# Attention then MLP on one core: all engines in program order, an opening written by hand, and batch 2 transposed on TensorE

## The chip, the cores and the metric

One core of a Trainium2 chip. The metric is the device time of the kernel in microseconds (us), the median of several runs; executions of one kernel mostly agree within 1%. An execution more than 1.5% above the fastest of the same kernel in its call is taken as slow and left out of ratios. The granted clock is the share of PE's full clock rate that the profile shows as granted: 1.00 is full, 0.50 half; "cold" means run at less than full clock. PE is the matmul engine TensorE, DVE is VectorE, ACT is ScalarE, POOL is GpSimd (here it mostly issues the loads), SP is SyncE (it issues stores and DMA transposes).

## The reference, cut to what matters

```python
# q, k, v: (8 batches, 8 heads, 576, 64); p: (8, 8, 32, 64); x = 4608 tokens of 512
def sm_attn(qq, kk, vv): ...          # softmax(scale * qq @ kk^T) @ vv
p_packed = sm_attn(p, k, v)           # 32 packed rows per head
out = sm_attn(q, p_packed, p_packed)
x = out.transpose(0, 2, 1, 3).reshape(4608, 512)
h = x @ w_in                          # 512 -> 2048
g = s * relu(h) ** 2 + b
y = g @ w_out                         # 2048 -> 512
```

## The kernel before

The kernel works batch by batch. For each batch it prepares k, q, v and p, computes the scores of p against k ("first scores"), the packed rows ("packed"), the scores of q against the packed rows ("second scores", then "weights"), and multiplies the packed rows by w_in beforehand ("packed_w"). Then 16 hidden steps follow: `mlp_in(b, m)` is four matmuls on PE, a ReLU on ACT and a squaring on DVE into `gT`. The output tiles of a batch (16 matmuls each) are spread over the hidden steps of the next batch, and so is the attention of the batch to come. In the profile lines, `pn` is p as loaded, `pbd`, `kT` and `qT` are the transposed p, k and q, `qr` and `vr` are copies of q and v in another order that DVE makes, `ppbd` holds the packed rows, `e` exponentials, `aT` the weights, `pw` the packed rows times w_in, `hps` and `yps` are PSUM tiles, and `rlu` is what the ReLU of a hidden step gives.

Only PE's instructions are held in program order. On the other engines the scheduler may move an instruction forward when it expects its inputs to be ready.

```python
kn/qn/vn: one buffer each (rawp, bufs=1);  qr, vr, e1, e2: one each (attp, bufs=1)
kT, qT, pbd, ppbd: two each, by b % 2;     PSUM: three "h" tiles, two "y" tiles

def mm(*a, **kw):
    return tc.keep_in_program_order(nc.tensor.matmul(*a, **kw))

def by_chunk(dst, src):                      # 96 x 3072 copy on DVE
    nc.vector.tensor_copy(...)
def order_q(b): qr[b] = attp.tile(...); by_chunk(qr[b], qn[b])
def order_v(b): vr[b] = attp.tile(...); by_chunk(vr[b], vn[b])
def dma_k(b):   nc.sync.dma_start_transpose(out=kT[b % 2]..., in_=kn[b]...)
def dma_q(b):   nc.sync.dma_start_transpose(out=qT[b % 2]..., in_=qr[b]...)

def prep_p(b):
    nc.vector.tensor_copy(out=pn[:, b, :, 1, :], in_=pn[:, b, :, 0, :])   # "the p copy"
    pt = big(BF16)
    for qd in range(NQ):
        tr(pt[...], pn[:, b, qd, :, :], identb[:])                        # PE
    ...                                                                   # two copies to pbd on DVE
# ... cut: per batch b of the loop, a = b + 1, c = b + 2
    steps[11]: dma_k(c), order_q(c), dma_q(c)        # batches 3 to 7; batch 2 at steps 4 and 6 of loop 1
    steps[14]: prep_p(c), order_v(c)
    for m in range(NFF):
        mlp_in(b, m)
        for f in steps.get(m, []): f()
        if b == 1 and m < 4: ...                     # 16 bias matmuls
        run_outs(todo, per)                          # 4 or 5 output matmuls of batch b - 1
```

The softmax here doesn't subtract the row's maximum and nothing guards it: scores larger than these inputs give would overflow.

## Time and profile before

| | before |
|---|---|
| time, median of 3 runs | 316.49 us (315.71 to 317.64) |
| profiled span | 312.5 us |
| PE busy | 255.1 us (82%) |
| mean granted clock of PE | 0.944 |

A page's slices cut the span in 40; each digit is the busy share in tenths. In an answer in order of time a line has the start, the duration, the engine, the source line, the operation with its output and inputs, and in brackets how long the engine stood idle before it and for what. In a table of waits the three numbers are the sum, the count and the longest. The lines of before stand in the prediction below.

### The profile page before, as it was taken

The numbers are of one execution on the slowest core, as the hardware profiler recorded it, in microseconds if no ns is written. First come the engines' busy times: TensorE is split into PE (matmuls) and PEld (weight loads), VectorE is DVE, ScalarE is ACT, GpSimd is POOL, SyncE is SP. The second block draws the span as 40 slices with busy tenths as digits, with TensorE's granted clock in tenths as the row PEclk, the third lists the DMA queues.
The fourth block names the chain that finished last, engine by engine and source line by source line (L and its number), as shares of the span: only waits on it lengthen the run. The fifth ranks groups of instructions, "written<-read, shape, count | busy, mean of one in ns | idle before, by whom it ended". The sixth has DMA issues, their size and how long they took to land.

```text
span 312.5 us, 4756 instructions
## 1 busy us (share of the span) xinstructions
PE 255.1 (82%) x1890; PEld 144.8 (46%) x1920; DVE 146.3 (47%) x291; ACT 140.4 (45%) x209; POOL 28.8 (9%) x40
## 2 busy tenths in 40 slices
PE   0286868239599469939999799999999999999994
PEld 0272554114265236514665455556556655555441
DVE  1354845250445073436554746563665447444211
ACT  1026655402155514525547654755585467444100
POOL 8341010001101001100010000000000000000000
PEclk9999996758799959997999999999999999999999
DMA  8999999999998975986279336721112111212132
GB/s 95 203 207 202 206 196 179 144 153 176 147 180 108 185 120 107 166 125 109 64 119 182 93 88 111 150 68 35 36 34 69 34 36 34 69 36 67 47 89 67
DMA packets 59240, 35.45 MB, mean 113 GB/s; under 512 B 32081, under 2 KB 54609, under 8 KB 59217
## 3 DMA queue, kind: packets, MB, share of 16 engines
q0 software_dynamic: 25136, 18.61, 41.1%
q1 hardware_dynamic: 34080, 16.52, 27.9%
q8 instruction: 15, 0.25, 0.3%
q14 instruction: 9, 0.07, 0.1%
HBM read 37.23 MB, written 9.44 MB: 149 GB/s over the span
## 4 chain that ended last, share of the span: by engine, by line
PE 58%; DMA 10%; DVE 4%; issue 1%; DVEq 0%
PE yps L72 35%; PE hps L72 23%; DMA qT<-qr 10%; DVE gT L384 1%; DVE pw L358 1%; DVE qr L165 0%; DVE ysb L428 0%; DVE aT L333 0%; DVE vr L165 0%; PE hps L75 0%; DVE biasrep L392 0%; DVE ppbd L288 0%; DVE pbd L177 0%; DVEq L165 0%
## 5 line engine op out<-in xcount | busy, mean ns | idle before, releaser
L72 PE MATMUL yps<-w_out_sb,gT 128*128 128x512 bf16 x547 | 141.7, 387 | 5.5 <-DVE biasrep L392 3.2
L382 ACT ACTIVATE rlu<-hps 128x576 bf16<-128x576 f32 x128 | 82.9, 650 | 126.9 <-PE hps L72 125.3
L72 PE MATMUL hps<-aT,pw 128*128 128x288 bf16 x512 | 88.6, 300 | 19.1 <-DVE aT L333 12.4
L384 DVE TENSOR_TENSOR gT<-rlu 128x576 bf16<-128x576 bf16 x128 | 58.0, 455 | 77.1 <-ACT rlu L382 76.4
L72 PEld LDWEIGHTS <-gT 128*128 128x128 bf16 x576 | 53.8, 99 | 58.0 <-issue 13.9
L72 PEld LDWEIGHTS <-pw 128*128 128x128 bf16 x512 | 51.5, 102 | 58.5 <-issue 22.6
L428 DVE SCALAR_TENSOR_TENSOR ysb<-yps,svec,biasrep 128x512 f32<-128x512 f32 x36 | 26.9, 747 | 14.1 <-PE yps L72 13.8
L72 PE MATMUL hps<-w_in_sb,ppbd 128*64 128x512 bf16 x128 | 19.4, 424 | 7.4 <-DVE pbd L177 7.0
L165 DVE COPY qr<-qn 96x3072 bf16<-96x3072 bf16 x8 | 7.6, 956 | 37.6 <-DMA qT<-qr 27.5
L358 DVE TENSOR_SCALAR pw<-hps,rd 128x1024 bf16<-128x1024 f32 x16 | 20.4, 1277 | 4.4 <-PE hps L72 4.3
L252 ACT ACTIVATE e<-hps 96x768 bf16<-96x768 f32 x16 | 12.7, 799 | 15.4 <-PE hps L72 15.4
L72 PEld LDWEIGHTS <-ppbd 128*64 128x64 bf16 x192 | 9.7, 117 | 20.3 <-DVE pbd L177 7.5
L356 ACT ACTIVATE pw<-hps,rd 128x1024 bf16<-128x1024 f32 x16 | 17.8, 1114 | 0.6 <-PE hps L72 0.6
L89 POOL DMA_DIRECT2D kn<-in_k_dram x9 | 8.3, 923 | 74.8 <-DMA kT<-kn 63.4
L72 PE MATMUL hps<-pbd,kT 128*128 128x64 bf16 x192 | 9.2, 202 | 5.6 <-DVE kT L193 5.6
L316 ACT ACTIVATE e<-hps,rs 128x576 bf16<-128x576 f32 x16 | 10.9, 737 | 6.1 <-PE hps L72 5.4
L333 DVE TENSOR_TENSOR aT<-e,rcd 128x576 bf16<-128x576 bf16 x16 | 11.8, 753 | 3.9 <-ACT rcd L332 3.6
L72 PEld LDWEIGHTS <-kT 128*128 128x128 bf16 x192 | 8.6, 104 | 6.8 <-DVE kT L193 5.9
L165 DVE COPY vr<-vn 96x3072 bf16<-96x3072 bf16 x8 | 7.7, 956 | 8.2 <-DMA vn<-in_v_dram 5.8
L75 PE MATMUL hps<-identb,pn 128*128 128x128 bf16 x16 | 2.4, 239 | 10.4 <-DVE pn L172 8.6
L72 PE MATMUL hps<-e,vr 96*128 96x64 bf16 x192 | 8.8, 199 | 2.4 <-DVE qT L223 2.4
L332 ACT ACTIVATE rcd<-ld 128x576 f32<-128x576 f32 x16 | 10.6, 684 | 0.3
(41 smaller groups left out, 109.1 us busy)
## 6 DMA issues: line engine op xcount, KB each, us to landing
qn<-in_q_dram POOLq DMA_DIRECT2D x8, 576.0 KB, 8.1
vn<-in_v_dram POOLq DMA_DIRECT2D x8, 576.0 KB, 11.3
out_dram<-ysb SPq DMA_DIRECT2D x24, 192.0 KB, 2.3
kn<-in_k_dram POOLq DMA_DIRECT2D x7, 576.0 KB, 8.8
out_dram<-ysb SPq DMA_DIRECT2D x24, 128.0 KB, 2.4
w_in_sb<-in_moe_w_in_dram POOLq DMA_DIRECT2D x4, 512.0 KB, 14.0
w_out_sb<-in_moe_w_out_dram POOLq DMA_DIRECT2D x4, 512.0 KB, 21.7
out_dram<-ysb SPq DMA_DIRECT2D x24, 64.0 KB, 2.0
```

The costliest lines, as they stand in the source:

```text
L72: return tc.keep_in_program_order(nc.tensor.matmul(*a, **kw))
L89: nc.gpsimd.dma_start(out=t[:, h0:h0 + step, :], in_=src[b, h0:h0 + step].rearrange("h (r c) d -> r h (c d)", c=NC),)
L165: nc.vector.tensor_copy(out=dst[:].rearrange("r c h d -> r h c d"), in_=src[:].rearrange("r h (c d) -> r h c d", c=NC),)
L252: nc.scalar.activation(out=e1[b][:, qd].rearrange("r c g j -> r g c j"), in_=s1[0:R].rearrange("r a (g x) -> r (a g) x", g=2)[:, :, 0:NC * ...
L316: nc.scalar.activation(out=e2[b][:, qd, :].rearrange("p (a s) -> p a s", a=2), in_=tiles[qd][:, :, 0:HS], func=AF.Exp, scale=rs[b][:, qd:q ...
L332: nc.scalar.activation(out=rcd[:], in_=ld[:].rearrange("p a s -> p (a s)"), func=AF.Exp, scale=-1.0)
L333: nc.vector.tensor_tensor(out=aT[b][:, qd, :], in0=e2[b][:, qd, :], in1=rcd[:], op=ALU.mult)
L356: nc.scalar.activation(out=dst, in_=tiles[qd][:], func=AF.Copy, scale=rd[b][:, qd:qd + 1])
L358: nc.vector.tensor_scalar_mul(out=dst, in0=tiles[qd][:], scalar1=rd[b][:, qd:qd + 1])
L382: nc.scalar.activation(out=rlu[:], in_=hps[:, :, 0:HS], func=AF.Relu)
L384: nc.vector.tensor_tensor(out=gT[:, m, g0:g0 + S].rearrange("p (a s) -> p a s", a=2), in0=rlu[:], in1=rlu[:], op=ALU.mult,)
L428: nc.vector.scalar_tensor_tensor(out=ysb[:], in0=self.yps[:], scalar=svec[:], in1=biasrep[:], op0=ALU.mult, op1=ALU.add,)
```

## The change

The intent: no engine is to stand behind an instruction that the scheduler moved too far forward, the opening is to use data as they land, and batch 2, whose DMA transposes fell into the heaviest loading, is to be transposed on PE.

```diff
+    class Pinned:
+        def __getattr__(self, name):
+            f = getattr(self.engine, name)
+            return lambda *a, **kw: tc.keep_in_program_order(f(*a, **kw))
+    vec, act, pool, sp = (Pinned(e) for e in (nc.vector, nc.scalar, nc.gpsimd, nc.sync))
 # ... every nc.vector., nc.scalar.activation, nc.gpsimd., nc.sync. becomes vec., act., pool., sp.
 # ... opening, after second_scores(0):
-    weights(0, 0); weights(0, 1); packed_w(0, 0)
+    packed_w1(0, 0); weights(0, 0); weights(0, 1); packed_w1(0, 1)
+    mlp_in(0, 0..5); packed_w1(0, 2); mlp_in(0, 6..7); packed_w1(0, 3); mlp_in(0, 8..12)
+    prep_k(1, 0); prep_k(1, 1); mlp_in(0, 13); mlp_in(0, 14)
+    first_scores(1, 0); first_scores(1, 1); mlp_in(0, 15)
+    order_q(1); prep_q(1, 0); prep_q(1, 1); order_v(1); packed(1, 0); packed(1, 1)
+    loads(2)
+    with_bias(0); second_scores(1); with_bias(4); weights(1, 0); weights(1, 1)
+    packed_w(1, 0); with_bias(8); packed_w(1, 1); with_bias(12)   # each: 4 bias + 4 output matmuls
-    for b in range(B):
+    for b in range(1, B):
 # ... batch 2 in loop 1: prep_p, prep_k, order_q, prep_q, order_v on PE and DVE, steps 2 to 10
-            if b == 1:
-                at = [8, 9, 10, 11, 12, 13, 14, 14, 15]
+                at = [2, 4, 5, 6, 7, 8, 10, 11, 12, 13, 14, 14, 15]
+        if b == 2:
+            steps[1]: order_q(3), dma_k(3), dma_q(3);  steps[3]: prep_p(3), order_v(3)
-            steps[11]: dma_k(c), order_q(c), dma_q(c);  steps[14]: prep_p(c), order_v(c)
+        if b >= 2: steps[13]: order_q(c), dma_k(c), dma_q(c);  steps[15]: prep_p(c), order_v(c)
```

(The last lines and the list of calls are shortened. Left out: the loads of the batch after next now stand at step 4 of a loop, in loop 1 at step 10, instead of ahead of it; the steps of the attention in loop 2 are spread anew; 8 output matmuls stand ahead of loop 2's first hidden step.)

All instructions that go through `Pinned` show its line, L82, in the profiles after; go by the tiles there.

More of the change, by code (lines that the diff above doesn't have):

```diff
@@ L5 @@
 from concourse import bass_utils, mybir
-from concourse.masks import make_identity
 from concourse._compat import with_exitstack
@@ L75, in tr, with __init__ @@
         return tc.keep_in_program_order(nc.tensor.transpose(*a, **kw))
+    class Pinned:
+        def __init__(self, engine):
+            self.engine = engine
+        def __getattr__(self, name):
+            f = getattr(self.engine, name)
+            return lambda *a, **kw: tc.keep_in_program_order(f(*a, **kw))
+    vec, act, pool, sp = (Pinned(e) for e in (nc.vector, nc.scalar, nc.gpsimd, nc.sync))
     def big(dt=F32):
@@ L88, in load @@
         for h0 in range(0, H, step):
-            nc.gpsimd.dma_start(
+            pool.dma_start(
                 out=t[:, h0:h0 + step, :],
@@ L99, in load_p @@
     def load_p(b0, b1):
-        nc.gpsimd.dma_start(
+        pool.dma_start(
             out=pn[:, b0:b1, :, 0, :],
@@ L105, in load_w_in @@
     def load_w_in(ch):
-        nc.gpsimd.dma_start(
+        pool.dma_start(
             out=w_in_sb[:, :, ch * NB:(ch + 1) * NB],
@@ L111, in load_w_out @@
     def load_w_out(m0, m1):
-        nc.gpsimd.dma_start(
+        pool.dma_start(
             out=w_out_sb[:, m0:m1, :],
@@ L115, in load_w_out @@
         )
+    identb = constp.tile([P, P], BF16, name="identb")
+    vec.memset(identb[:], 0.0)
     load(kn, k, 0, "kn", parts=2)
@@ L119 @@
     load(qn, q, 0, "qn")
+    pool.affine_select(
+        out=identb[:], in_=identb[:], compare_op=ALU.not_equal, fill=1.0, base=0,
+        pattern=[[-1, P]], channel_multiplier=1,
+    )
     load(vn, v, 0, "vn")
     svec = constp.tile([P, 1], F32, name="svec")
-    nc.sync.dma_start(out=svec[:], in_=moe_s[0:1].unsqueeze(0).to_broadcast([P, 1]))
+    sp.dma_start(out=svec[:], in_=moe_s[0:1].unsqueeze(0).to_broadcast([P, 1]))
     bvec = constp.tile([P, 1], F32, name="bvec")
-    nc.sync.dma_start(out=bvec[:], in_=moe_b[0:1].unsqueeze(0).to_broadcast([P, 1]))
+    sp.dma_start(out=bvec[:], in_=moe_b[0:1].unsqueeze(0).to_broadcast([P, 1]))
     nc.scalar.preload_act_table_set("natural_log_exp_and_others")
-    identb = constp.tile([P, P], BF16, name="identb")
-    nc.vector.memset(identb[:], 0.0)
-    make_identity(nc, identb, nomemset=True)
     for ch in range(NCH):
@@ L139 @@
     for i in range(2):
-        nc.vector.memset(pbd[i][:], 0.0)
-        nc.vector.memset(kT[i][:, H * HS:KW], 0.0)
+        vec.memset(pbd[i][:], 0.0)
+        vec.memset(kT[i][:, H * HS:KW], 0.0)
     ones1 = constp.tile([P, 1], BF16, name="ones1")
-    nc.vector.memset(ones1[:], 1.0)
+    vec.memset(ones1[:], 1.0)
     for i in range(2):
-        nc.vector.memset(ppbd[i][:], 0.0)
+        vec.memset(ppbd[i][:], 0.0)
     onesbd = constp.tile([P, P], BF16, name="onesbd")
-    nc.vector.memset(onesbd[:], 0.0)
+    vec.memset(onesbd[:], 0.0)
     for g in range(4):
-        nc.vector.memset(onesbd[NP * g:NP * g + NP, NP * g:NP * g + NP], 1.0)
+        vec.memset(onesbd[NP * g:NP * g + NP, NP * g:NP * g + NP], 1.0)
     onesb = constp.tile([P, P], BF16, name="onesb")
-    nc.vector.memset(onesb[:], 1.0)
+    vec.memset(onesb[:], 1.0)
     biasrep = constp.tile([P, NB], F32, name="biasrep")
@@ L164, in by_chunk @@
     def by_chunk(dst, src):
-        nc.vector.tensor_copy(
+        vec.tensor_copy(
             out=dst[:].rearrange("r c h d -> r h c d"),
@@ L171, in prep_p @@
         i = b % 2
-        nc.vector.tensor_copy(out=pn[:, b, :, 1, :], in_=pn[:, b, :, 0, :])
+        vec.tensor_copy(out=pn[:, b, :, 1, :], in_=pn[:, b, :, 0, :])
         pt = big(BF16)
@@ L176, in prep_p @@
         for c2 in range(2):
-            nc.vector.tensor_copy(
+            vec.tensor_copy(
                 out=pbd[i][D * c2:D * c2 + D, :, :, c2, :],
@@ L192, in prep_k @@
                 )
-        nc.vector.tensor_copy(
+        vec.tensor_copy(
             out=kT[i][:, half * 4 * HS:(half + 1) * 4 * HS].rearrange("p (a s) -> p a s", a=2),
@@ L198, in dma_k @@
     def dma_k(b):
-        nc.sync.dma_start_transpose(
+        sp.dma_start_transpose(
             out=kT[b % 2][:, 0:H * HS].rearrange("p (x r) -> p x r", r=R),
@@ L222, in prep_q @@
                 )
-        nc.vector.tensor_copy(
+        vec.tensor_copy(
             out=qT[i][:, CP * half:CP * half + CP, :, :].rearrange("p c h r -> p (c h r)").rearrange(
@@ L230, in dma_q @@
     def dma_q(b):
-        nc.sync.dma_start_transpose(
+        sp.dma_start_transpose(
             out=qT[b % 2][:].rearrange("p c h r -> p (c h) r"),
@@ L251, in first_scores @@
                 )
-        nc.scalar.activation(
+        act.activation(
             out=e1[b][:, qd].rearrange("r c g j -> r g c j"),
@@ L287, in packed @@
             for h2 in range(2):
-                nc.vector.tensor_copy(
+                vec.tensor_copy(
                     out=ppbd[i][D * h2:D * h2 + D, :, NP * h2:NP * h2 + NP],
@@ L294, in packed @@
             rd[b] = smp.tile([P, NQ], F32, tag="rd", name="rd")
-            nc.vector.reciprocal(out=rd[b][:], in_=pp[:, 1, 0:NQ])
+            vec.reciprocal(out=rd[b][:], in_=pp[:, 1, 0:NQ])
             rs[b] = smp.tile([P, NQ], F32, tag="rs", name="rs")
-            nc.vector.tensor_scalar_mul(out=rs[b][:], in0=rd[b][:], scalar1=scale)
+            vec.tensor_scalar_mul(out=rs[b][:], in0=rd[b][:], scalar1=scale)
     def second_scores(b):
@@ L315, in second_scores @@
         for qd in range(NQ):
-            nc.scalar.activation(
+            act.activation(
                 out=e2[b][:, qd, :].rearrange("p (a s) -> p a s", a=2),
@@ L329, in weights @@
         ld = smp.tile([P, 2, HS], F32, tag="ld", name="ld")
-        nc.scalar.activation(out=ld[:], in_=dps[:, :, 0:HS], func=AF.Ln)
+        act.activation(out=ld[:], in_=dps[:, :, 0:HS], func=AF.Ln)
         rcd = smp.tile([P, S], F32, tag="rcd", name="rcd")
-        nc.scalar.activation(out=rcd[:], in_=ld[:].rearrange("p a s -> p (a s)"), func=AF.Exp, scale=-1.0)
-        nc.vector.tensor_tensor(out=aT[b][:, qd, :], in0=e2[b][:, qd, :], in1=rcd[:], op=ALU.mult)
+        act.activation(out=rcd[:], in_=ld[:].rearrange("p a s -> p (a s)"), func=AF.Exp, scale=-1.0)
+        vec.tensor_tensor(out=aT[b][:, qd, :], in0=e2[b][:, qd, :], in1=rcd[:], op=ALU.mult)
     def packed_w(b, c2):
@@ L355, in packed_w, with packed_w1 @@
             if qd == 0:
-                nc.scalar.activation(out=dst, in_=tiles[qd][:], func=AF.Copy, scale=rd[b][:, qd:qd + 1])
+                act.activation(out=dst, in_=tiles[qd][:], func=AF.Copy, scale=rd[b][:, qd:qd + 1])
             else:
-                nc.vector.tensor_scalar_mul(out=dst, in0=tiles[qd][:], scalar1=rd[b][:, qd:qd + 1])
+                vec.tensor_scalar_mul(out=dst, in0=tiles[qd][:], scalar1=rd[b][:, qd:qd + 1])
+    def packed_w1(b, ch):
+        i = b % 2
+        if ch == 0:
+            pw[b] = ppw.tile([P, NQ, DFF], BF16, tag="pw", name="pw")
+        t = big()
+        for qd in range(NQ):
+            for pr in range(2):
+                hp = 2 * qd + pr
+                mm(
+                    t[64 * pr:64 * pr + 64, qd, :],
+                    ppbd[i][:, hp, :],
+                    w_in_sb[:, hp, ch * NB:(ch + 1) * NB],
+                    start=True,
+                    stop=True,
+                    tile_position=(0, 64 * pr),
+                )
+        dst = pw[b][:, :, ch * NB:(ch + 1) * NB]
+        act.activation(out=dst[:, 0], in_=t[:, 0, :], func=AF.Copy, scale=rd[b][:, 0:1])
+        vec.tensor_scalar_mul(out=dst[:, 1], in0=t[:, 1, :], scalar1=rd[b][:, 1:2])
     def slot(b):
@@ L381, in mlp_in @@
         rlu = ysp.tile([P, 2, HS], BF16, tag="rlu", name="rlu")
-        nc.scalar.activation(out=rlu[:], in_=hps[:, :, 0:HS], func=AF.Relu)
+        act.activation(out=rlu[:], in_=hps[:, :, 0:HS], func=AF.Relu)
         g0 = slot(b) * S
-        nc.vector.tensor_tensor(
+        vec.tensor_tensor(
             out=gT[:, m, g0:g0 + S].rearrange("p (a s) -> p a s", a=2),
@@ L391, in bias_part @@
         if m == NFF - 1:
-            nc.vector.tensor_scalar_mul(out=biasrep[:], in0=cps[:], scalar1=bvec[:])
+            vec.tensor_scalar_mul(out=biasrep[:], in0=cps[:], scalar1=bvec[:])
     def store(ysb, i0, b, col, n):
@@ L400, in store @@
             m = min(R - r0, end - i0)
-            nc.sync.dma_start(out=rows[c, r0:r0 + m, :], in_=ysb[i0:i0 + m, :])
+            sp.dma_start(out=rows[c, r0:r0 + m, :], in_=ysb[i0:i0 + m, :])
             i0 += m
@@ L427, in step @@
                 ysb = ysp.tile([P, NB], F32, tag="ysb", name="ysb")
-                nc.vector.scalar_tensor_tensor(
+                vec.scalar_tensor_tensor(
                     out=ysb[:], in0=self.yps[:], scalar=svec[:], in1=biasrep[:],
@@ L454, in run_outs, with loads @@
                 todo.pop(0)
+    def loads(b):
+        load(kn, k, b, "kn")
+        load(qn, q, b, "qn")
+        load(vn, v, b, "vn")
     prep_p(0)
@@ L469, with with_bias @@
     second_scores(0)
+    packed_w1(0, 0)
     weights(0, 0)
     weights(0, 1)
-    packed_w(0, 0)
-    for b in range(B):
+    packed_w1(0, 1)
+    for m in range(0, 6):
+        mlp_in(0, m)
+    packed_w1(0, 2)
+    for m in range(6, 8):
+        mlp_in(0, m)
+    packed_w1(0, 3)
+    for m in range(8, 13):
+        mlp_in(0, m)
+    prep_k(1, 0)
+    prep_k(1, 1)
+    mlp_in(0, 13)
+    mlp_in(0, 14)
+    first_scores(1, 0)
+    first_scores(1, 1)
+    mlp_in(0, 15)
+    order_q(1)
+    prep_q(1, 0)
+    prep_q(1, 1)
+    order_v(1)
+    packed(1, 0)
+    packed(1, 1)
+    loads(2)
+    cps = psy.tile([P, NB], F32, tag="y", name="yps")
+    todo = outs(0)
+    def with_bias(m0):
+        for m in range(m0, m0 + 4):
+            bias_part(cps, m)
+        run_outs(todo, 4)
+    with_bias(0)
+    second_scores(1)
+    with_bias(4)
+    weights(1, 0)
+    weights(1, 1)
+    packed_w(1, 0)
+    with_bias(8)
+    packed_w(1, 1)
+    with_bias(12)
+    for b in range(1, B):
         a = b + 1
@@ L489 @@
             at = [0, 1, 3, 4, 6, 8, 9, 10, 12]
-            if b == 0:
+            if b == 1:
                 seq = [
+                    lambda: prep_p(a),
                     lambda: prep_k(a, 0),
@@ L494 @@
                     lambda: (order_q(a), first_scores(a, 0)),
-                    lambda: first_scores(a, 1),
-                    lambda: (prep_q(a, 0), prep_q(a, 1)),
+                    lambda: (first_scores(a, 1), prep_q(a, 0)),
+                    lambda: prep_q(a, 1),
                     lambda: (order_v(a), packed(a, 0)),
                 ] + seq[3:]
-                at = [7, 8, 9, 10, 11, 12, 13, 14, 15, 15, 15, 15]
-            if b == 1:
-                at = [8, 9, 10, 11, 12, 13, 14, 14, 15]
+                at = [2, 4, 5, 6, 7, 8, 10, 11, 12, 13, 14, 14, 15]
+            if b == 2:
+                at = [4, 5, 6, 7, 9, 10, 11, 12, 13]
             for s, f in zip(at, seq):
                 steps.setdefault(s, []).append(f)
-        if a + 1 < B:
-            c = a + 1
-            load(kn, k, c, "kn")
-            load(qn, q, c, "qn")
-            load(vn, v, c, "vn")
-            steps.setdefault(11, []).append(lambda: (dma_k(c), order_q(c), dma_q(c)))
-            steps.setdefault(14, []).append(lambda: (prep_p(c), order_v(c)))
-            if b == 0:
-                steps[11].pop()
-                steps[14].pop()
-        if b == 1:
-            steps.setdefault(4, []).insert(0, lambda: (dma_k(2), order_q(2), dma_q(2)))
-            steps.setdefault(6, []).insert(0, lambda: (prep_p(2), order_v(2)))
-        todo = outs(b - 1) if b > 0 else []
+        if b == 2:
+            steps.setdefault(1, []).append(lambda: (order_q(3), dma_k(3), dma_q(3)))
+            steps.setdefault(3, []).append(lambda: (prep_p(3), order_v(3)))
+        c = a + 1
+        if b >= 2 and c < B:
+            steps.setdefault(13, []).append(lambda: (order_q(c), dma_k(c), dma_q(c)))
+            steps.setdefault(15, []).append(lambda: (prep_p(c), order_v(c)))
+        if b > 1:
+            todo = outs(b - 1)
         per = len(todo)
-        if b == 1:
-            cps = psy.tile([P, NB], F32, tag="y", name="yps")
+        if b == 2:
+            run_outs(todo, 8)
         for m in range(NFF):
-            if b == 0 and m == NFF // 2:
-                packed_w(0, 1)
+            if c < B and m == (10 if b == 1 else 4):
+                loads(c)
             mlp_in(b, m)
@@ L526 @@
                 f()
-            if b == 1 and m < 4:
-                for x in range(4):
-                    bias_part(cps, 4 * m + x)
             run_outs(todo, per)
+        run_outs(todo, NFF * (NT + 1))
     todo = outs(B - 1)
```

## The prediction

> **What bounds the kernel now.** I read the page's busy shares and slices first, then the waits of TensorE (PE), then the order of time on VectorE (DVE) where the long waits end, then the chain that ended last for the price of one piece of PE work.
>
> Page, busy shares and the 40 slices of 7.8 us:
> ```profile
> PE 255.1 (82%) x1890; PEld 144.8 (46%) x1920; DVE 146.3 (47%) x291; ACT 140.4 (45%) x209; POOL 28.8 (9%) x40
> ...
> PE   0286868239599469939999799999999999999994
> ...
> PEclk9999996758799959997999999999999999999999
> DMA  8999999999998975986279336721112111212132
> ```
> PE is the only engine near its limit, and from the 24th slice (180 us) on it is full: nothing is to be gained there. The holes and the low clock lie before, in the first 140 us, and the DMA engines are full for the first 94 us.
>
> Waits of PE (waited for, us in total, times, longest):
> ```profile
> PE hps L72 <- DVE aT L333: 12.4, 2, 10.3
> PE hps L75 <- DVE pn L172: 8.6, 1, 8.6
> PE hps L72 <- DVE pbd L177: 7.0, 1, 7.0
> PE hps L72 <- DVE pw L358: 5.6, 2, 5.3
> PE hps L72 <- DVE kT L193: 5.6, 1, 5.6
> PE yps L72 <- DVE biasrep L392: 3.2, 1, 3.2
> ```
> All name DVE, which is busy 47%. So it is DVE's order, not its load. In DVE's order of time:
> ```profile
> 8.30 0.30 DVE L172 COPY pn<-pn 128x128 bf16<-128x128 bf16 x2 [5.86 <-DMA pn<-in_p_dram]
> 11.27 0.96 DVE L165 COPY qr<-qn 96x3072 bf16<-96x3072 bf16 x1 [2.67 <-DMA qn<-in_q_dram]
> 14.14 0.96 DVE L165 COPY vr<-vn 96x3072 bf16<-96x3072 bf16 x1 [1.92 <-DMA vn<-in_v_dram]
> 15.01 0.58 DVE L177 COPY pbd<-hps 64x256 bf16<-64x256 bf16 x2
> 15.63 1.42 DVE L193 COPY kT<-hps 128x1152 bf16<-128x1152 bf16 x2
> ...
> 64.54 0.95 DVE L165 COPY qr<-qn 96x3072 bf16<-96x3072 bf16 x1 [8.07 <-DMA qT<-qr]
> 65.42 1.27 DVE L358 TENSOR_SCALAR pw<-hps,rd 128x1024 bf16<-128x1024 f32 x1
> 66.61 1.41 DVE L333 TENSOR_TENSOR aT<-e,rcd 128x576 bf16<-128x576 bf16 x2
> ```
> pbd and kT need only k and p, in by 8.3, but stand behind the copies of q and v, so the first scores start at 16.4. At 64.5 the copy for a batch two ahead waits 8.07 us for the DMA transpose reading the single qr buffer, with pw and aT, which PE needs now, behind it: that is the 10.3. The same copy makes the 7.0 (ends 112.1), the 5.3 (140.6) and a 1.6 (179.5). The 3.2 is the first output tile behind biasrep, behind yet another waiting copy (80.3).
>
> Chain, late pieces:
> ```profile
> 217.03 0.97 PE hps L72 x22
> ...
> 222.09 1.10 PE hps L72 x12
> ...
> 225.51 1.47 PE hps L72 x12
> ...
> 239.12 0.84 PE hps L72 x16
> ...
> 274.74 0.49 PE hps L72 x4
> 275.23 0.86 PE yps L72 x4
> ```
> Warm prices: one hidden step (4 matmuls) 0.49; 4 output matmuls 0.86 (0.215 each); less the 0.49 of their hidden step, 12 first scores 0.35, 18 packed 0.48, 8 second scores 0.61, 8 of packed times w_in 0.98.
>
> **What the Trainium skill says.** "TensorE: Matmul & The Clock Gate", section "Part 1: The HAM clock gate": an idle window of about 3.4 us halves PE's clock, and a busy one of that length restores it. The trace agrees: granted clock 0.58 from 57 to 67.4, and the first hidden step after it takes 1.31 against 0.65 warm. Same page, "Architectural detail": ScalarE (ACT) and DVE queues are strict FIFO. The two waits above show it: nothing passes a waiting copy. "DMA: Bandwidth & Descriptors", "Issuing engines are not separate DMA queues": all DMAs interleave on the same 16 engines. The trace agrees: a qT transpose takes 9.4 us from 164.3, when loads are few, and 15.3 from 49.2, under them.
>
> **The change part by part.**
>
> (1) Order. The diff drops no arithmetic; each engine now follows the text. A waiting q copy of batch 4 to 7 stands at step 13, one batch after the previous transpose of q was issued, so qr is long free. Gone: 10.3 + 7.0 + 5.3 + 1.6 + 3.2 = 27.4 us of PE waits, and cold clock after them: from 67.4 to 79.4 the clock is 0.79, from 82.7 to 104.5 0.92, from 112.1 to 135.3 0.90, from 140.6 to 164 0.93, so about 2.5 + 1.7 + 2.3 + 1.6 = 8.1 us. These two overlap with what DMA may ask back.
>
> (2) Opening. Loads are issued in the same order, so they land as before. Landings I read from who waits: p 8.3, q0 11.2, v0 14.1; the pool issues that wait for w_in give its four pieces as about 16.9, 19.5, 22.0, 25.6; q1 30.7, v1 33.6, the rest of p 45.1 (hence w_out's pieces 36 to 44). That is 2.9 us per 576 KB, about 200 GB/s. Replay with the durations of before:
> - PE starts at 8.56 as now. pbd and kT are done by 11.7 (2 x 0.29 and 2 x 0.75 behind 2.1 us of transposes) instead of 17.0; first scores 11.7 to 13.2; q copied 11.7 to 12.6, transposed and copied to 16.3; v copied to 17.2; packed to 19.0; second scores 19.7 (22.6 before).
> - From second scores to the first hidden step there remain two exps, one half-sized pw, two ld and two rcd on ACT, then aT: 0.7 + 0.7 + 0.7 + 0.6 + 4 x 0.65 + 0.75, near 6 us. First hidden step 25.7, against 29.4.
> - Batch 0's 16 hidden steps have no output work beside them, so ACT sets the pace: four cold ones 0.96, then 0.65 to 0.7, plus three pw pieces of 0.6: 12 to 13 us. The transposes and first scores of batch 1 come in between (about 4 us); order_q, prep_q, order_v and packed of batch 1 run after the last step, one after another (5 to 6 us). Packed of batch 1 ends near 47.
> - 16 bias and 16 output matmuls (32 x 0.215 = 6.9), second scores, weights and w_in products (0.61 + 0.49 + 1.96), two or so of waits for PSUM behind ACT: the first hidden step of batch 1 falls near 58, against 67.4, and with 6.9 us of later work already done.
>
> (3) Batch 2 on PE. Adds 48 transposes (24 took 1.37 us: 2.7) and four copies of 0.75 on DVE; removes two of twelve DMA transposes, those under the heaviest load traffic. Its loads are queued by 46 and land at 48, 51 and 54, before they are used.
>
> (4) Sum. Attention of one batch costs PE 2 x 0.35 + 2 x 0.48 + 0.61 + 0.49 + 1.96 + 0.1 = 4.8. Loop 1: 16 x 0.49 + 48 x 0.215 + 4.8 + 2.7 = 25.6, ends 83.6, one more for ACT's crowded last steps: 84.5. Loops 2, 4, 6 (80 output matmuls): 7.8 + 17.2 + 4.8 = 29.9; loops 3 and 5 (64): 26.5; loop 7: 21.7; tail of 80: 17.3; end of last output matmul to end of span as before, 4.2. 84.5 + 3 x 29.9 + 2 x 26.5 + 21.7 + 17.3 + 4.2 = 270. New waits: 3 (below). Span 273, against 312.5. The timed median of before lies 4 above its profiled span, the profiled run 1.8, so I add 3: 276.
> As a check: loops from 212.1 to 290.2 took 78.1 in the profile; my prices give 26.5 + 29.9 + 21.7 = 78.1.
>
> **The rivals.**
> A. The transposes become the new wait. In loop 2 k and q of batch 3 are sent at step 1 (near 88); kT needs 5.4 (118.71 to 124.06), qT 9.4 to 11.9 behind it, so 103 to 106, just when step 9 wants it (near 104), and batch 4's loads collide. In loop 4, stores are ahead of batch 6's transposes on the sync queue and three steps (5 us) may not cover kT. For: strict order means PE stops; against: most are sent 16 us ahead. My 3 us are for this; if each qT takes 12 and loads stretch kT too, some 2 us more in four or five loops: 285.
> B. DMA stays the bound in the opening, so the order gains nothing. For: DMA is full till 94. Against: all 18.6 MB of loads take 91 us at 205 GB/s, PE's work for the first three batches reaches past 84, and DVE waits for its own order while data lie ready. If batches 2 and 3 came late, 285 to 290.
> C. Strict order on DVE and ACT costs small PSUM waits in the full loops, where the scheduler's order left PE 99% busy. 1 us in each of six loops: 282.
> D. Only the four big waits go and the opening gains nothing: 316.5 - 27.4 - 8.1 + 2.7 = 284.
> E. The opening goes better than the replay (warm clock, ACT overlapping more): 268.
>
> **Range and chances.** The rivals give 268 to 290, singly. Central 276; 266 to 287 holds 8 in 10. For 310, 34 of the 40 us would have to come back: faster 0.97, within 2% 0.02, slower 0.01.
>
> **What would show it.** No DVE copy of q waiting for qT's DMA; first scores near 12; first hidden step of batch 0 near 26, of batch 1 near 58; loop 2 starting near 85; PE idle in all 22 to 32 us instead of 57, PE busy about 248; granted clock above 0.96; full loops of 26.5 and 29.9. Wrong if PE waits over 3 us for kT or qT at steps 0, 6 or 9, if the loads of batch 2 land after 58, or if full loops lengthen by a microsecond or more.

## More of the kernel before

One line of before is from DVE's order of time:

```profile
45.14 0.70 DVE L172 COPY pn<-pn 128x128 bf16<-128x128 bf16 x6 [3.35 <-DMA pn<-in_p_dram]
```

## The result, and the profile after

| | before | after |
|---|---|---|
| time, median of 4 runs | 316.25 us (315.71 to 317.64) | 291.67 us (290.88 to 292.27) |
| ratio | | 0.9215, 95% interval 0.9175 to 0.9255 |
| profiled span | 312.5 us | 290.5 us |
| PE busy | 255.1 us | 252.1 us |
| mean granted clock | 0.944 | 0.970 |

A ratio here is the mean time of one kernel's fast runs over that of the other's of the same rounds, so not quite the ratio of the medians. The direction was right; the time lies 4.7 us above the stated range and 15.7 above the stated 276.

The page after, the slices of PE and of its clock:

```profile
PE   0667857989699899979997999799989999999993
...
PEclk9999985999889999979999999999999999999999
```

The hole of before at slices 8 and 9 is gone, and so is much of the low clock of slices 7 to 19, but small dips to 7 or 8 stand in PE's row at intervals up to slice 30. Before, the row was full from slice 24 on. What makes them, in the waits of PE after:

```profile
PE hps L74 <- DVE pn L82: 17.6, 8, 9.2
PE hps L71 <- DVE vr L82: 5.5, 3, 2.1
PE hps L74 <- DVE qr L82: 2.8, 2, 2.6
...
PE hps L71 <- DMA kT<-kn: 1.2, 3, 0.5
```

No wait of 5 us or more is left but the first, for p at the start. The wait for `pn` is new in count: eight times instead of once. Less the 9.2 at the start and a 0.27 it is six waits of 1.34 to 1.45 us, 8.1 us in all. One of them, first PE and then DVE in their order of time:

```profile
97.81 0.65 PE L71 MATMUL hps<-aT,pw 128*128 128x288 bf16 x4
99.80 0.29 PE L74 MATMUL hps<-identb,pn 128*128 128x128 bf16 x2 [1.34 <-DVE pn L82]
```
```profile
99.18 0.46 DVE L82 TENSOR_TENSOR gT<-rlu 128x576 bf16<-128x576 bf16 x1 [0.79 <-ACT rlu L82]
99.56 0.19 DVE L82 COPY pn<-pn 128x128 bf16<-128x128 bf16 x1
```

The p copy needs nothing but p, in since 45 us. In strict order it stands on DVE behind the squaring of the hidden step just ahead, which waits for that step's ReLU on ACT (98.50 to 99.15), which waits for the matmuls. PE's transposes of p stand directly behind those matmuls. So PE waits for a whole round from PE over ACT and DVE back to PE: 1.34 us, in each of loops 1 to 5, twice in loop 2. Before, the scheduler had made all six copies in one go at 45.1 us.

Where time went against the prediction, with PE's first hidden step of each batch as the mark:

| stage | predicted us | measured us |
|---|---|---|
| start to first hidden step of batch 1 | 58 | 59.4 |
| loop 1 and the first 8 output matmuls of loop 2 | 28.2 | 33.7 |
| rest of loop 2 | 28.2 | 31.8 |
| loop 3 | 26.5 | 30.7 |
| loop 4 | 29.9 | 32.2 |
| loop 5 | 26.5 | 29.1 |
| loop 6 | 29.9 | 30.2 |
| loop 7, tail and end | 43.2 | 43.5 |
| waits put in apart | 3 | |

The clock, by stages (columns: stretch, its length, busy time and instructions of PE, weight loads, DVE, ACT and POOL, granted clock, DMA share, GB/s), loops 1 and 3 after; loops 2 and 4 had 1.00:

```profile
59.40:93.10 33.70, 29.29 (x255) 17.54 (x258) 19.73 (x37) 17.39 (x26) 2.31 (x3) 0.95 0.45 77
...
124.90:155.60 30.70, 28.37 (x216) 16.22 (x220) 16.89 (x35) 17.43 (x26) 2.29 (x3) 0.94 0.78 137
```

Loops 1 and 3 ran partly at a low clock, some 1.7 and 1.8 us (33.7 x 0.05 and 30.7 x 0.06). The longest stretch of low clock lies in the opening: 0.50 from 40.8 to 51.0 us, some 5 us lost (10.2 x 0.5), within a stage that came out only 1.4 us over its price.

### The profile page after: what moved, and what is told of

The parts are those of the page before. It is cut to its first block, busy times and chain, and to the rows that moved or that the text cites. A ratio compares the mean times of both kernels' runs of the same rounds, so it can differ in the third digit from the quotient of the medians.

```text
span 290.5 us, 4848 instructions
## 1 busy us (share of the span) xinstructions
PE 252.1 (87%) x1937; PEld 145.3 (50%) x1968; DVE 151.2 (52%) x297; ACT 140.5 (48%) x211; POOL 27.6 (10%) x40
## 4 chain that ended last, share of the span: by engine, by line
PE 76%; DMA 8%; ACT 6%; DVE 6%; issue 3%; POOL 0%; ACTq 0%; POOLq 0%
PE yps L71 42%; PE hps L71 31%; DMA kT<-kn 6%; ACT rlu L82 4%; PE hps L74 3%; DMA pn<-in_p_dram 2%; DVE gT L82 1%; DVE qr L82 1%; DVE vr L82 1%; ACT e L82 1%; ACT ld L82 1%; DVE kT L82 1%; ACT rcd L82 1%; DVE qT L82 1%; DVE ysb L82 0%
## 5 line engine op out<-in xcount | busy, mean ns | idle before, releaser
L71 PE MATMUL yps<-w_out_sb,gT 128*128 128x512 bf16 x547 | 140.1, 383 | 2.4 <-issue 1.1
L82 ACT ACTIVATE rlu<-hps 128x576 bf16<-128x576 f32 x128 | 82.2, 651 | 96.3 <-PE hps L71 86.0
L82 DVE TENSOR_TENSOR gT<-rlu 128x576 bf16<-128x576 bf16 x128 | 58.4, 456 | 83.7 <-ACT rlu L82 83.0
L71 PE MATMUL hps<-aT,pw 128*128 128x288 bf16 x512 | 83.4, 288 | 2.4 <-DVE aT L82 1.5
L71 PEld LDWEIGHTS <-pw 128*128 128x128 bf16 x512 | 50.2, 99 | 38.2 <-issue 5.3
L82 DVE SCALAR_TENSOR_TENSOR ysb<-yps,svec,biasrep 128x512 f32<-128x512 f32 x36 | 26.9, 747 | 16.0 <-PE yps L71 15.7
L82 DVE TENSOR_SCALAR pw<-hps,rd 128x1024 bf16<-128x1024 f32 (+1 forms) x18 | 20.8, 1159 | 2.9 <-ACT pw L82 2.8
L82 POOL DMA_DIRECT2D kn<-in_k_dram x9 | 7.2, 797 | 138.4 <-DMA kT<-kn 81.3
L82 DVE TENSOR_TENSOR aT<-e,rcd 128x576 bf16<-128x576 bf16 x16 | 12.1, 758 | 15.1 <-ACT rcd L82 15.0
L82 ACT ACTIVATE e<-hps,rs 128x576 bf16<-128x576 f32 x16 | 10.9, 738 | 17.7 <-PE hps L71 17.7
L71 PE MATMUL hps<-w_in_sb,ppbd 128*64 128x512 bf16 x128 | 18.3, 396 | 1.0 <-ACT ld L82 0.5
L82 ACT ACTIVATE pw<-hps,rd 128x1024 bf16<-128x1024 f32 (+1 forms) x18 | 18.3, 1019 | 0.3 <-PE hps L71 0.2
L82 ACT ACTIVATE e<-hps 96x768 bf16<-96x768 f32 x16 | 12.6, 800 | 11.7 <-PE hps L71 11.6
L71 PE MATMUL hps<-e,vr 96*128 96x64 bf16 x192 | 9.9, 209 | 5.5 <-DVE vr L82 5.5
L71 PEld LDWEIGHTS <-vr 96*128 96x128 bf16 x192 | 8.9, 108 | 6.9 <-DVE vr L82 6.3
L82 ACT ACTIVATE rcd<-ld 128x576 f32<-128x576 f32 x16 | 10.9, 683 | 0.5
L82 ACT ACTIVATE ld<-hps 128x576 f32<-128x576 f32 x16 | 10.3, 643 | 1.0 <-PE hps L71 1.0
```

The source lines that it names most:

```text
L82: return lambda *a, **kw: tc.keep_in_program_order(f(*a, **kw))
```

## The experiments

Theory: strict order removed the waits as predicted, but made new ones where the text puts a copy on DVE directly ahead of its reader on PE (p in six places, v and q of batch 2), some of them followed by cold clock; and batch 2 on PE costs more than its matmuls. Rivals: the DMA transposes are the new wait; strict order on DVE and ACT costs a little everywhere; the opening gained nothing. All runs gave the right result. The runs, each beside runs of the kernel before on the same chip (its medians there: 315.18, 315.06 and 314.19). In the third call, the last four lines of the table, four of the seven runs of before were slow and only three (309.35 to 312.02) count; the record marks all four verdicts of that call as unclear, so these ratios are not to be laid beside those of the other calls to a per cent:

| run | time us | ratio to before | 95% interval | span us | clock |
|---|---|---|---|---|---|
| the change | 291.67 | 0.9215 | 0.9175 to 0.9255 | 290.5 | 0.970 |
| p copies early | 287.58 | 0.9163 | 0.908 to 0.9245 | 285.3 | 0.972 |
| order only (part 1) | 290.06 | 0.9237 | 0.9169 to 0.9304 | 288.0 | 0.976 |
| text only (parts 2, 3) | 298.38 | 0.9495 | 0.9421 to 0.9569 | 296.5 | 0.954 |
| batch 2 by DMA (parts 1, 2) | 284.43 | 0.9048 | 0.8983 to 0.9114 | 282.7 | 0.988 |
| p early, transposes at step 11 | 281.96 | 0.8950 | 0.8894 to 0.9007 | 281.1 | 0.972 |
| v of batch 2 early | 287.99 | 0.9126 | 0.9065 to 0.9188 | 287.0 | 0.978 |
| batch 2 by DMA, p early, step 11 | 276.68 | 0.8772 | 0.8722 to 0.8822 | 273.4 | 0.988 |
| the same, opening copies early | 268.33 | 0.8513 | 0.8473 to 0.8553 | 266.1 | 0.998 |
| before, two qr buffers | 311.02 | 0.9996 | 0.9928 to 1.0064 | 310.0 | 0.934 |
| before, DVE in order | 291.75 | 0.9365 | 0.9284 to 0.9446 | 287.9 | 0.975 |
| the change, filled gap | 289.74 | 0.9314 | 0.9234 to 0.9394 | 287.2 | 0.980 |
| before, all but DVE in order (median with one slow run; fast runs 306.63 to 310.52) | 309.41 | 0.9915 | 0.9787 to 1.0043 | | |

### 1. The p copies early

```diff
 # prep_p(b)
-        vec.tensor_copy(out=pn[:, b, :, 1, :], in_=pn[:, b, :, 0, :])
+        if b < 2:
+            vec.tensor_copy(out=pn[:, b, :, 1, :], in_=pn[:, b, :, 0, :])
 # opening, after packed(1, 1)
+    for x in range(2, B):
+        vec.tensor_copy(out=pn[:, x, :, 1, :], in_=pn[:, x, :, 0, :])
```

> The changed kernel, with the second copy of p of batches 2 to 7 made in one go on DVE in the opening (after packed of batch 1, when all of p has landed) instead of inside each batch's preparation; nothing else moves. Theory 1 (my lost time is a copy that strict order puts just before its use: in six loops PE waits 1.34 to 1.45 us for it, 8.1 us, and the clock drops after some of these gaps): all six waits go, PE waits for the p copy only at the start, time falls by 8 to 12 us from 291.7 to 280 to 284. Rival (the kT transposes are the new wait, and the p copies only hide it): the 1.34 waits turn into waits for kT of the same length, time 289 to 292. Rival (strict order on DVE and ACT costs many small waits): 288 to 290.

Measured: 287.58 us. That is a smaller gain than expected, and its interval overlaps that of the change, so the time alone proves nothing. The waits of PE do:

```profile
PE hps L74 <- DVE pn L82: 8.9, 2, 8.7
PE hps L71 <- DMA kT<-kn: 6.5, 4, 2.1
```

All six p waits are gone, and the waits for the DMA transpose of k, issued at step 13 and read at step 0 of the next loop, grew from 1.2 to 6.5 us: 5.3 of the 8.1 came back. Loop 2, which has two p waits and no kT wait behind them, shortened by just their sum, 31.8 to 29.0 (first ReLU to first ReLU). So both the theory and rival A of the prediction hold, side by side: the p wait hid the kT wait. Loop 1 went from 33.7 to 30.8: its p wait is gone, and in this execution its clock was 1.00 (run 12 comes back to that).

### 2. Order only

The kernel before, with its own text, and all five engines in program order (the edit is the `Pinned` class alone).

> The kernel before with its own text, all engines in program order (part 1 alone; batch 2 by DMA transpose, opening unchanged). If the order as such is worth the 27.4 us of waits that my prediction gave it: 285 to 292. If the old text in strict order has waits of its own (loads, order of q and transposes at step 4 of loop 1 just before their use), it gains little or loses: 305 to 325. I expect the second, near 308: in the old text the transposes of batch 2 and the scores that need them stand four steps apart, and a transpose took 5 to 15 us.

Measured: 290.06 us, ratio 0.9237, the same as the whole change within the intervals. My expectation of 308 was wrong, and the prediction's 27.4 us of waits for part 1 is near the net gain of 25. That it is so near is partly chance: the clock was to give more, and the new waits below, which it did not have, took that back. The old text in order even has the early start of batch 0: its first ReLU runs at 26.9 us, against 26.6 in the change and 30.6 before. So the order alone brings that gain, which the prediction gave to the opening; run 3 shows that the new text alone brings it too. It has the p waits too, and in loop 1, where the old text crowds the end of a batch's attention, PE waits for DVE's pw and then again for the p copy:

```profile
85.47 0.41 PE L71 MATMUL hps<-e,onesbd 128*128 128x288 bf16 x2 [3.19 <-DVE pw L82]
88.23 0.40 PE L74 MATMUL hps<-identb,pn 128*128 128x128 bf16 x2 [2.35 <-DVE pn L82]
```

### 3. Text only

The text of the change with `Pinned` handing instructions on unpinned.

> The text of the changed kernel with only PE in program order, as before the change (parts 2 and 3 without part 1). If the order is what removes the waits of the q copy behind the qT transpose, they come back for batches 4 to 7: two to four waits of 2 to 7 us, time 293 to 305; but the p copies are hoisted again, so PE waits for them only at the start, which gives back 8. I expect 292 to 300.

Measured: 298.38 us, ratio 0.9495, inside the expected range. The p copy is waited for once only, at the start, and the waits of DVE's q copy are back, four of them behind qT's transposes (26.4 us in all on DVE), with 10.13 and 6.45 us of waits of PE. Without the order the new text gives some two thirds of the gain. The two overlap, as order alone gave as much as all three parts: the first ReLU of batch 0 runs at 25.3 us here, without any order but PE's.

### 4. Batch 2 by DMA again

```diff
-                seq = [prep_p(a), prep_k(a, 0), prep_k(a, 1), (order_q(a), first_scores(a, 0)), ...]
-                at = [2, 4, 5, 6, 7, 8, 10, 11, 12, 13, 14, 14, 15]
+                at = [8, 9, 10, 11, 12, 13, 14, 14, 15]
+        if b == 1:
+            steps.setdefault(2, []).append(lambda: (order_q(2), dma_k(2), dma_q(2)))
+            steps.setdefault(4, []).append(lambda: (prep_p(2), order_v(2)))
```

> The changed kernel with batch 2 transposed by DMA again (issued at step 2 of loop 1, used from step 8; part 3 undone). My prediction held part 3 to cost 2.7 us of PE and to save waits under load. If transposes of batch 2 are hidden: 289 to 291 (2.7 us of PE work gone, a p-copy wait as before). If they are late, as rival A of the prediction has it: PE waits 3 to 12 us for kT or qT in loop 1, time 294 to 304. I expect the second, 296.

Measured: 284.43 us, ratio 0.9048, clear of the change's. I had expected the transposes to be late; they were not, as the DMA engines stood nearly idle ahead of them (1 tenth busy in the page's slice from 57 to 64 us). Loop 1 of this run:

```profile
60.20:87.80 27.60, 25.57 (x209) 14.79 (x212) 17.01 (x34) 17.39 (x26) 2.29 (x3) 1.00 0.79 136
```

27.6 us at full clock, against 33.7 at 0.95. Transposing batch 2 on PE costs 6.1 us of loop 1 instead of the 2.7 of its matmuls. Together with run 2 this puts the three parts on the scale of time, if they are added in this sequence (run 3 shows that they overlap): order about -25 us, the new text without batch 2 about -6 more, batch 2 on PE about +5 to +7 (1.0185, the ratio of the two ratios, is 5.3 us; the medians differ by 7.2). The middle share is that of the opening and of the moves inside the loops together; they were not run apart.

### 5. Both waits away

Run 1 and, besides, for the batch after next:

```diff
-            steps.setdefault(13, []).append(lambda: (order_q(c), dma_k(c), dma_q(c)))
+            steps.setdefault(11, []).append(lambda: (order_q(c), dma_k(c), dma_q(c)))
```

> The changed kernel with the p copies early (as in the run before) and, from loop 2 on, the copy of q and both DMA transposes of the batch after next at step 11 instead of 13. In the run with early p copies alone the six p waits (8.1 us) went, but PE waited 6.5 us for kT in loops 3 to 6 instead of 1.2. Theory 2 (two waits lie side by side: the p copy and kT; whichever is taken away uncovers the other): both gone, so 287.6 less 6.5 and less 1.8 of cold clock in loop 3: 279 to 281, no kT wait over 0.3. Rival (kT is late because the DMA engines are busy, whatever its place): kT waits of 1 to 2 us stay, 285 to 288.

Measured: 281.96 us, ratio 0.8950. PE waits for kT no more, and from loop 3 on the loops took 28.3, 30.8, 27.2 and 30.7 us. The low clock of loop 3 went too, but as much came in loop 1 (0.95, where run 1 had 1.00), so the mean stayed at 0.972, and the time is 1 us above the expected range. A third wait also came to light: PE now waits for DVE's `pbd`, three times, 2.1 us in all, up to 1.33; it is in runs 7 and 8 as well. The DMA engines were not too busy; the transposes stood too close to their reader.

### 6. v of batch 2 early

```diff
-                    lambda: prep_k(a, 1),
+                    lambda: (prep_k(a, 1), order_v(a)),
-                    lambda: (order_v(a), packed(a, 0)),
+                    lambda: packed(a, 0),
```

> The changed kernel with one move: the copy of v of batch 2 at step 5 of loop 1 instead of at step 10, directly ahead of packed that reads it. Theory: the 2.1 us wait before packed goes, and with it the cold clock after it (1.7 us by the clock of 0.95 over that loop): 287.5 to 290. Rival (the cold clock there has another cause): 289.5 to 290. If it does nothing, the wait was covered by another: 291 to 292.

Measured: 287.99 us, ratio 0.9126 (against 0.9215; the intervals overlap by a little). Loop 1 shortened from 33.7 to 30.9 us, first ReLU to first ReLU. So of the 6 us that batch 2 on PE cost, near 3 went with one copy placed directly ahead of its reader; the clock of the loop is 1.00 here, with all the transposes still in it. At full clock PE is busy for 27.76 us in this loop and for 25.57 in that of run 4: the matmuls of part 3 cost 2.2 us, near the 2.7 of the prediction. The other 1.1 of the 3.3 that are left is a new wait for ACT's `e` (1.07).

### 7. All three

Run 4 with the edits of runs 1 and 5.

> Batch 2 by DMA (part 3 undone), early p copies, transposes at step 11. From the run with batch 2 by DMA (284.4, six p waits of 8.1 us still in it, kT waits 0.8): if taking away waits adds up, 284.4 less 8.1 less 0.8: 275 to 277, which is what the prediction said of the change itself. If kT or qT becomes the new wait: 279 to 283.

Measured: 276.68 us, span 273.4. The waits add up. This is near the 276 that the prediction gave for the change, but without part 3, which it had priced at 2.7, and with waits and low clock in the opening that it did not have; that the two numbers meet is partly chance.

### 8. The opening too

```diff
-    load(kn, k, 0, "kn", parts=2)
     load_p(0, 2)
+    load(kn, k, 0, "kn", parts=2)
-    prep_q(0, 0); prep_q(0, 1); order_v(0)
+    prep_q(0, 0); order_v(0); prep_q(0, 1)
     mlp_in(0, 13)
+    order_q(1)
     mlp_in(0, 14)
+    order_v(1)
 # ... and both gone from their places after mlp_in(0, 15)
```

> As the run before in this call, and in the opening: p loaded ahead of k, the copies of q and v of batch 1 made during the hidden steps of batch 0, the copy of v of batch 0 between the two halves of q's transposition. Expected if the waits in the opening for those copies (2.65, 1.72 and 1.72 us) and the wait for p at the start (8.7 to 9.2) are on the path: p about 1.5 us earlier, 4 us from batch 1, 1 us from batch 0: 6 us below the run before, near 270. Rival (w_out's landing or ACT sets the end of the opening): 1 to 3 us below.

Measured: 268.33 us, ratio 0.8513, 8.3 us below run 7, more than expected. This is the version to keep: it beats the change by 23 us. At the start p now lands first, but then k is waited for, so little comes of that: the first ReLU of batch 0 runs at 25.7 us, against 26.5 in run 7:

```profile
5.01 0.40 PE L74 MATMUL hps<-identb,pn 128*128 128x128 bf16 x2 [5.01 <-DVE pn L82]
7.47 1.14 PE L74 MATMUL hps<-identb,kn 96*128 96x96 bf16 x12 [2.06 <-DMA kn<-in_k_dram]
```

The greater share is the stretch from batch 0's first ReLU to batch 1's: 25.7 us instead of 32.2, with the waits for the copies of q and v of batch 1 gone (2.65 and 1.72 us in run 7). Run 7 also had the clock at 0.50 from 41.5 to 48.3 us, behind the first of them, and run 8 has 1.00 there, which is worth 3.4 us. The mean clock is 0.998. The three edits of this run were not run apart.

### 9. Before, with two qr buffers

```diff
-        qr[b] = attp.tile([R, NC, H, D], BF16, tag="qr", name="qr")
+        qr[b] = atp.tile([R, NC, H, D], BF16, tag="qr", name="qr")    # bufs=2
```

> The kernel before, with two qr buffers in place of one and nothing else. If what cost it was the q copy waiting on DVE for the transpose that reads the one buffer, the waits of 10.3, 7.0, 5.3 and 1.6 us and most of the cold clock go without any order: 316 less 24 to 32, so 284 to 292. Rival (the copy then waits for the next thing, the landing of q, at the same place on DVE): 298 to 312.

Measured: 311.02 us, ratio 0.9996: nothing, the rival's end of the range. From DVE's order of time, two of its q copies:

```profile
81.59 0.96 DVE L165 COPY qr<-qn 96x3072 bf16<-96x3072 bf16 x1 [11.87 <-DMA qn<-in_q_dram]
...
110.68 0.95 DVE L165 COPY qr<-qn 96x3072 bf16<-96x3072 bf16 x1 [6.34 <-DMA qT<-qr]
```

With a second buffer the copy, still as far forward, waits for the landing of q or for the transpose before the last. The single buffer that the wait named was not what cost the time; that it was the place in DVE's order, run 10 shows.

### 10 and 11. Which engine's order

Run 2 with only DVE (and PE) in order, and with all but DVE in order.

> The kernel before with only DVE (and PE, as before) in program order. All engines in order, with the same text, gave 290.1. If DVE's order is what counts: 288 to 293. If the order of ACT or of the loads has a share: 294 to 308.

> The kernel before with ACT, POOL and SP (and PE) in program order, DVE left to the scheduler. If only DVE's order counts: 312 to 318, the waits behind the q copy as before. If the loads' order or ACT's has a share: 300 to 310.

Measured: 291.75 us, ratio 0.9365, with DVE alone; 309.41, ratio 0.9915, not to be told from 1, with all but DVE. DVE's order gives most of the gain. With DVE alone the interval (0.9284 to 0.9446) still touches that of all engines (0.9169 to 0.9304), so by time a share of the others is possible but not shown. The traces leave little room for one: the spans are 287.9 and 288.0 us, and the first ReLU of each of batches 2 to 7 runs within 0.2 us of the same moment (batch 2 at 94.7 in both, batch 7 at 245.3 and 245.4).

### 12. The gap filled

```diff
-                    lambda: (order_v(a), packed(a, 0)),
+                    lambda: (order_v(a), fill(8), packed(a, 0)),   # 8 matmuls of 512 columns, result unused
```

> The changed kernel with eight bias-shaped matmuls of 512 columns into an unused PSUM tile, issued on PE between the copy of v of batch 2 and packed, so that they run (1.7 us) in the 2.1 us wait at step 10 of loop 1; the outputs are right. If the clock of 0.95 in loop 1 comes from that gap: wait for v down to 0.4 or so by the trace, packed at the same moment, but warm after it: clock of loop 1 near 1.0, time 1.5 to 2 us below 291.7. If the clock is low for another reason: 291 to 292.

Measured: 289.74 us by the median, but its ratio to before is 0.9314, so by time the run is inconclusive. In the trace the wait for v is 0.38 instead of 2.10, and packed after it, 12 matmuls, takes 0.52 instead of 0.82. The same matmuls in the change, here, and in run 1:

```profile
78.46 0.82 PE L71 MATMUL hps<-e,vr 96*128 96x64 bf16 x12 [2.10 <-DVE vr L82]
...
77.81 0.52 PE L71 MATMUL hps<-e,vr 96*128 96x64 bf16 x12 [0.38 <-DVE vr L82]
...
76.54 0.52 PE L71 MATMUL hps<-e,vr 96*128 96x64 bf16 x12 [2.10 <-DVE vr L82]
```

The clock of loop 1 is 1.00 instead of 0.95, and the loop 32.3 us instead of 33.7, though PE did 1.9 us more work in the gap. That alone would put the low clock down to the gap. But run 1 has the same gap of 2.10 us at the same place, unfilled, and its matmuls are warm and its loop at 1.00; run 5 has the gap and 0.95 again. So with this gap, two of three profiled executions were cold for some 3.4 us after it, and none of the five without it (runs 4, 6, 7, 8 and this one). The gap seems to be needed, it is not enough, and what decides is not shown. For loop 3 it is no clearer: in the change two waits of 1.45 and 0.48 us lie close together there and the clock was 0.94; in run 4 two waits of 1.45 and 0.41 lie there and the clock was 1.00.

## Why the prediction was wrong

**What bounds the kernel, and part 1: right.** DVE's order was what cost, not its load. Order alone gave the gain (run 2), and DVE's order most of it (runs 10 and 11). One reading was too narrow: the waits named the single qr buffer, and freeing it does nothing (run 9).

**Part 2, the replay: right in its times, wrong in what it credits.** First hidden step of batch 0 predicted 25.7, measured 24.9; of batch 1, 58 and 59.4. But for the early start of batch 0 the opening was not needed: order brings it with the old text (run 2), and the new text brings it without order (run 3). And the second number holds 10.2 us at half clock that the replay did not have, so that it came so near is partly luck.

**The step that failed: "(4) Sum", which prices strict order at nothing.** I took away the waits that order removes and put in 3 us of new ones, for kT and qT. I did not walk through the new text for places where a DVE copy stands between a hidden step and its reader on PE. Measured: six p waits, 8.1 us; the copies of v and q of batch 2, 2.3 us; kT 1.2 us; cold clock in loops 1 and 3, 3.5 us; opening 1.4 us net. That is 16.5 of the 20.1 us by which the span of 290.5 exceeds the 270.4 of the sum without its new waits. The other 3.6 are gaps too short to be listed one by one; about 0.4 us a loop of this stood in the loops of before already (30.3 and 26.9 for loops 4 and 5, against prices of 29.9 and 26.5). The prediction's check of its prices, 78.1 us for loops 5 to 7 of before, did not show it, as its price for loop 7 is 0.7 too high (21.7 against 21.0) and the errors cancel. Of the signs of being wrong that the prediction named, the last one came: full loops were 2.3 to 4.2 us longer than priced in loops 3 to 5. The 1.8 us between profiled run and span were as before, where I had added 3.

**Part 3: mis-sized.** The 2.7 us of matmuls were near right as such (2.2 by runs 4 and 6), but the loop pays 6.1 (run 4). The rest is the copies of v and q ahead of their readers (2.3 us of waits) and 1.7 of low clock in that execution. Nor did it save a wait: the transposes of batch 2 by DMA are hidden once the order is right, as the heavy loading is over by then (in run 4; in run 10, with the old text, PE waits once for it, 2.08 us for qT).

**The rivals.** A named the right place, three steps not covering kT, but the p wait stood ahead of it and hid most of it: 1.2 us as changed, 6.5 with the p waits gone (run 1), none two steps earlier (run 5). qT was never late in the change: it took 4.9 to 7.5 us there from issue to landing. The 9.4 us that the prediction had for it "when loads are few" was misread: in those 9.4 us two loads were under way, and the DMA moved 210 GB/s in all. C came nearest: 1 us in each of six loops, where there were six waits of 1.34 to 1.45 us, but they are for p, not for PSUM. B did not happen: the loads of batch 2 were in before their use. D, with 284, assumed that the opening gains nothing; the change came out slower still. The range was too narrow above because it treated these as alternatives, while A's wait and one of C's size came together.

## What to carry to other kernels

An order that keeps an early instruction from blocking a late one also keeps an early one from running ahead: when an engine is put in strict order, look in the trace for what the scheduler had hoisted, and move that in the text by hand to where its inputs are ready. Where a producer stands directly behind the work of the engine that will read it, that engine pays a full round over the others (1.34 us here). Move such a producer forward: two hidden steps were enough for the copies of q and v of batch 1 (run 8); whether one is was not tested. And take waits away in pairs: behind a wait removed there may stand one of nearly the same length, as kT behind p here, so a small gain is no proof that the wait was not real.

## What the Trainium skill lacked or had wrong

- "TensorE: Matmul & The Clock Gate", the table "Why this matters for your kernels", advises no idle gaps over about 3 us between bursts. Here a gap of 2.10 us was followed by some 3.4 us at half clock in two profiled executions (12 matmuls in 0.82 and 0.85 us instead of 0.52), and by full clock in a third (run 1). So a gap below 3 us is not always safe; what decides it is not shown.
- "DMA: Bandwidth & Descriptors", section "Latency and other measured facts", gives DMA transposes an effective 261 GB/s for a non-contiguous middle dimension, and about 350 to 400 for the contiguous case. Here a transpose of 96 x 3072 two-byte elements (0.59 MB) took 4.8 us from issue to landing at the quickest in any kept run, 123 GB/s, and 9.4 us (164.3 to 173.7 in the kernel before) beside two loads, 63 GB/s.
- No page gives the cost of a strictly ordered producer just ahead of its reader: 1.34 us per round of PE, ACT, DVE and back to PE with these tiles.
- No page says that a wait in a trace can hide another of nearly its length behind it: removing 8.1 us of waits for p gave 5.3 back as waits for kT.
